# A decode kernel whose last columns of wq are loaded row by row: wider rows, other DMA engines, and part of the loads from GpSimd's queue

## The chip, the cores and the metric

One core of one Trainium2 chip runs the kernel. The metric is the device time of one execution in microseconds (us), lower is better. The engines are TensorE (PE), VectorE (DVE), ScalarE (ACT), GpSimd (POOL) and SyncE (SP); data moves between HBM and SBUF by 16 DMA engines, which loads issued from any of these queues use.

## The reference

A decode step for 8 sequences: layer norm, grouped attention over the last 2048 positions of a cache, an output projection, and a small mixer with a feed-forward part, each with a residual. For one token per sequence the shifted mixer parts are zero, so `w1` and `w2` are not needed.

```python
def _A_ref(x, k_cache, v_cache, wq, wo):         # x (8, 1, 512)
    q = (x @ wq).reshape(B, Sq, 32, 128)...       # wq (512, 4096), bf16
    k, v = the last 2048 positions of each cache  # (8, 8, 2048, 128) each, shared by 4 heads
    p = _softmax(einsum("bhqd,bhkd->bhqk", q, k) * 128 ** -0.5)
    return einsum("bhqk,bhkd->bhqd", p, v)... @ wo

def _B_ref(x, w1, w2, w3, w4):
    x1 = x + hs                                   # hs is zero for S == 1
    return x1 + _gelu(_layernorm(x1) @ w3) @ w4

h = x + _A_ref(_layernorm(x), ...)
return h + _B_ref(_layernorm(h), ...)
```

## The kernel before

**What is moved.** K and V together are 64 MB, in 32 tiles of 2 MB (128 partitions of 16 KB). With wq, wo, w3 and w4 the kernel reads 79.18 MB. All large loads are issued by SP, in an order written out by hand: `wq`, then K, K, K, V, K, V, K and so on, `wo` in three pieces, `w3`, and `w4` in three pieces. There are three buffers for K tiles and three for V tiles, so an SP issue for a later tile waits until PE is done with the tile that had its buffer.

**Order of work.** Each engine runs its own list of operations in the order in which `op` was called; waits are semaphore values. The beginning of the lists is this: POOL clears tiles (`memset`), makes `iota_f`, and computes `rstd` for the layer norm (lines 231 and 232), after DVE's statistics of x (229, 230). DVE makes `xln_b` from it (234), then constants out of `ident_f` (237 to 252), then copies the transposed x (`xlnT`). PE multiplies it by `wq` (`pe_q`), the result is evicted to `qrow2` (323, 326) and turned (`q_turn`). Only then PE transposes the first K tiles (`pe_T`, line 383), and the attention runs on in a pipeline: transposed K (`evict`), scores (`pe_QK`), softmax, P times V (`pe_PV`), batch by batch. The end is the output projection, the layer norm, `w3`, gelu, `w4` (line 732) and the store.

**How wq lies in SBUF.** The 512 rows of wq are laid as four consecutive rows to a partition, 128 partitions, in `wbig`. The last `QF` columns of the last of these four rows are not loaded with the rest. These 128 short rows are loaded by several small loads into another tile, `wqF`, which uses room that w3 takes later. `FILL` lists them: number k, the group of partitions, and the slot n among `NF` = 3 slots of `wqF`. A load with k covers 4k rows. Because these rows lie in other partitions than the rest of wq, PE needs the matching elements of x in the same order: DVE copies them out (`xlnP`, line 282), PE transposes them (`pe_fT`), DVE copies them to `xlnF` (292), and `pe_qF` adds the products of `xlnF` and `wqF` to those of `pe_q`, in the same PSUM bank `S_ps`.

In the list before, `QF` is 1152 (rows of 2304 bytes), there are six small loads, all on SP's queue behind the large one, and only bank 1 of the two needs `pe_qF`. Line 207 is the line in the helper `dma` under which all loads stand.

Of the kernel before, what the change touches and what calls it, by code (L numbers as in the profile page):

```python
# [21 lines left out]
F = 1792  # L22
FC = F // 128
FG = FC // 2
KC = D // 128
EPS = 1e-5
# [53 lines left out]
def bass_sequential_preLN__sliding_block_cached__mixer_s_mlp__decode_kernel(  # L80
# [23 lines left out]
    with es:  # L104
        sb = lambda shape, dtype, name: es.enter_context(nc.sbuf_tensor(name, shape, dtype))
        ps_t = lambda shape, dtype, name: es.enter_context(nc.psum_tensor(name, shape, dtype))
        S = lambda name: es.enter_context(nc.semaphore(name))


        iota_f = sb([128, 128], dt.float32, "iota_f")  # L110
        ident_f = sb([128, 128], dt.float32, "ident_f")
        ident_b = sb([128, 128], dt.bfloat16, "ident_b")
# [8 lines left out]
        w3_sb = sb([128, KC, F], dt.bfloat16, "w3_sb")  # L121
        w4_sb = sb([128, FC, D], dt.bfloat16, "w4_sb")
# [19 lines left out]
        xlnF = sb([KF, NF, 32], dt.bfloat16, "xlnF")  # L142
        xlnP = sb([B, 4 * sum(k for k, _, _ in FILL)], dt.bfloat16, "xlnP")
        wqF = w3_sb[0:KF, 2:4, :].rearrange("p a n -> p (a n)")[:, 0:NF * QF].rearrange("p (s n) -> p s n", s=NF)
        xlnT = sb([128, KC, 32], dt.bfloat16, "xlnT")
        qrow = sb([128, 2, 512], dt.bfloat16, "qrow")

# [1 line left out]
        qblk = sb([128, 2, G, 2, QE], dt.bfloat16, "qblk")  # L149
# [46 lines left out]

        sem_k = [S(f"sem_k{i}") for i in range(NK)]
        sem_v = [S(f"sem_v{i}") for i in range(NV)]
        sem_wf = S("sem_wf")
# [5 lines left out]
        def dma(eng, dst, src, sem, *waits):  # L205
            def f(e):
                e.dma_start(dst, src).then_inc(sem, 16)  # L207
            eng.op(f, *waits, inc=False)


        dma(AC, x_sb[:], A_x.rearrange("b s d -> (b s) d"), sem_x)
# [9 lines left out]
        e_ones = PO.op(lambda e: e.memset(ones_f[:], 1.0))  # L221
        e_mz = PO.op(lambda e: e.memset(mblk[:], 0.0))
        e_lz = PO.op(lambda e: e.memset(lblk[:], 1.0))
        e_qz = PO.op(lambda e: e.memset(qblk[:], 0.0))
        e_warm = AC.op(lambda e: e.activation(scratch[:, 1:2], scratch[:, 0:1], ACT.Exp), e_scr)

        e_idb = DV.op(lambda e: e.tensor_single_scalar(ident_b[:], iota_f[:], 0.0, ALU.is_equal), e_iota)
        e_idf = DV.op(lambda e: e.tensor_single_scalar(ident_f[:], iota_f[:], 0.0, ALU.is_equal))
        e = DV.op(lambda e: e.bn_stats(st6[:, :], x_sb[:, :]), X)
        e = DV.op(lambda e: e.bn_aggr(mv[:, :], st6[:, :]), e)  # L230
        e = PO.op(lambda e: e.tensor_scalar(rstd[:, :], mv[:, 1:2], EPS, None, ALU.add), e)
        e = PO.op(lambda e: e.tensor_tensor(rstd[:, :], rstd[:, :], half[0:B, 0:1], ALU.pow), e)
# [36 lines left out]
        qT_ps = (o_rows, sm)  # L269
        fT_ps = pT_ps[:, 128:128 + NF * B]  # L270

        def fills():
            at = 0
            for k, h, n in FILL:
                yield k, slice(32 * h, 32 * h + 4 * k), n, at, slice(at, at + 4 * k)
                at += 4 * k

        def q_rows():
            for k, rows, n, at, where in fills():
                a = xln_b[:, :]  # L280
                cols = bass.AP(tensor=a.tensor, offset=a.offset + KC * at + KC - 1, ap=[a.ap[0], [KC, k], [KC * k, 4]])
                e_xP = DV.op(lambda e, cols=cols, where=where: e.tensor_copy(
                    xlnP[:, where].rearrange("b (e a) -> b e a", a=4), cols))

            def pe_fT(e):
                for k, rows, n, at, where in fills():
                    ins = e.matmul(fT_ps[rows, n * B:(n + 1) * B], xlnP[:, where], ident_b[0:B, 0:B],
                                   is_transpose=True, tile_position=(0, rows.start))
                return ins
            e = PE.op(pe_fT, e_xP)  # L290
            for k, rows, n, at, where in fills():
                e_fT = DV.op(lambda e, rows=rows, n=n: e.tensor_copy(xlnF[rows, n, 0:B], fT_ps[rows, n * B:(n + 1) * B]),
                             e, e_fz)
            out = []
            for j in range(2):
                def pe_q(e, j=j):
                    for kc in range(KC):
                        for u in range(4):
                            n = (4 * j + u) * R * DH
                            size = R * DH if kc < KC - 1 else max(0, min(R * DH, H * DH - QF - n))  # L300
                            if size:
                                ins = e.matmul(S_ps[j][32 * u:32 * (u + 1), 0:size], xlnT[:, kc, :], wq_v[:, kc, n:n + size],  # L302
                                               start=(kc == 0), stop=(kc == KC - 1 and size == R * DH),
                                               tile_position=(0, 32 * u), skip_group_check=True)
                    return ins

                def pe_qF(e):
                    for n in range(NF):
                        for u in range(4):
                            w = (u - 4) * R * DH + QF  # L310
                            lo = max(0, -w)
                            if lo < R * DH:
                                ins = e.matmul(S_ps[1][32 * u:32 * (u + 1), lo:R * DH], xlnF[:, n, :],
                                               wqF[:, n, w + lo:w + R * DH], start=False, stop=(n == NF - 1),
                                               tile_position=(0, 32 * u), skip_group_check=True)
# [12 lines left out]
                out.append(e)  # L328
            return out, e_q
# [431 lines left out]
        def load_wq():  # L761
            size = KC * H * DH - QF
            dma(SP, wbig[:, 0:size], A_wq.rearrange("(p k) n -> p (k n)", k=KC)[:, 0:size], sem_wq)
            for k, rows, n, at, where in fills():
                dma(SP, wqF[rows, n, :],
                    bass.AP(tensor=A_wq.tensor, offset=A_wq.offset + (KC * at + KC - 1) * H * DH + H * DH - QF,
                            ap=[[KC * H * DH, k], [KC * k * H * DH, 4], [1, QF]]), sem_wf, e_wz if n else None)
# [59 lines left out]
```

## Time and profile before

| | |
|---|---|
| median of 3 runs | 192.94 us (192.86 to 194.09) |
| the profiled execution | 193.02 us, its span 191.6 us |
| PE busy | 153.1 us (80%) |
| DVE, ACT, POOL busy | 116.5, 95.6, 13.7 us |
| read from HBM | 79.18 MB, 413 GB/s over the span |
| DMA queue of SP (q1) | 97.3% of 16 engines' span |

Times in the profile are counted from the start of the span. A row of the timeline gives start, length, engine, line, operation, output and inputs, number of instructions, and in brackets how long the engine had been idle and what released it. A row of the chain that ended last gives start, length and what ran. "SPq" is an issue of a load by SP; it is not the moving of the data. "DMA share" and the digits of the DMA line tell how busy the 16 DMA engines were.

### The profile page before, as it was taken

To read this page: it belongs to the slowest core of one execution; us is meant where nothing else is said; L and a number is where in the kernel's file an instruction comes from. 1 tells how busy PE (TensorE), PEld (TensorE's weight loads), DVE (VectorE), ACT (ScalarE), POOL (GpSimd) and SP (SyncE) were. 2 spreads that over 40 slices of the span, in tenths; PEclk is the share of its full clock that TensorE was granted. 3 is DMA by queue.
4 is the path that set the end of the run, shared out by engine and by line. 5 is a ranking of instruction groups with operands and counts; after the bars stand their busy time and mean duration, and the time that the engine had idled before them with its cause. 6 is when DMAs were issued, how large, how long until landed. Compare 5 with 4: busy or idle time off the path is not lost.

```text
span 191.6 us, 3183 instructions
## 1 busy us (share of the span) xinstructions
PE 153.1 (80%) x1326; PEld 94.7 (49%) x1333; DVE 116.5 (61%) x259; ACT 95.6 (50%) x124; POOL 13.7 (7%) x37
## 2 busy tenths in 40 slices
PE   0049999598988988699978887889798895797895
PEld 0013866375556554465555455545554562343552
DVE  2733455834499368655885587558855886657423
ACT  3002667638357727284469255924782676340341
POOL 8400200100010001000100010002000000000040
PEclk9999999957999999789999999999999999699999
DMA  6999999999999999999999999999999999999991
GB/s 224 452 400 431 434 414 434 438 429 431 428 424 434 424 434 434 433 421 431 431 434 421 434 434 434 424 431 428 429 428 431 438 424 431 428 431 415 413 406 74
DMA packets 6477, 79.38 MB, mean 414 GB/s; under 512 B 688, under 2 KB 704, under 8 KB 1856
## 3 DMA queue, kind: packets, MB, share of 16 engines
q1 hardware_dynamic: 6448, 79.18, 97.3%
q8 instruction: 10, 0.16, 0.3%
q14 instruction: 3, 0.02, 0.0%
q10 hardware_dynamic: 16, 0.01, 0.0%
HBM read 79.18 MB, written 0.01 MB: 413 GB/s over the span
## 4 chain that ended last, share of the span: by engine, by line
DMA 55%; PE 20%; SPq 8%; DVE 8%; ACT 6%; issue 1%
DMA knat<-in_A_k_cache_dram 29%; DMA vnat<-in_A_v_cache_dram 11%; DMA w_sb<-in_B_w_dram 10%; SPq L207 8%; PE kT_ps L383 8%; DMA wbig<-in_A_wq_dram 6%; ACT kT_sb L393 3%; ACT pT_sb L472 3%; PE o_rows L504 3%; PE S_ps L504 3%; DVE kT_sb L395 2%; PE S_ps L302 2%; DVE oacc L516 2%; PE S_ps L408 2%; DVE omask L514 1%
## 5 line engine op out<-in xcount | busy, mean ns | idle before, releaser
L393 ACT ACTIVATE kT_sb<-kT_ps 128x1024 bf16<-128x1024 bf16 x64 | 65.6, 1025 | 54.9 <-PE kT_ps L383 54.7
L383 PE MATMUL kT_ps<-turn_f,knat 128*128 128x128 f32 x512 | 77.1, 291 | 13.8 <-DMA knat<-in_A_k_cache_dram 8.7
L383 PEld LDWEIGHTS kT_ps<-turn_f,knat 128*128 128x128 f32 x512 | 59.5, 147 | 35.0 <-issue 13.0
L395 DVE COPY kT_sb<-kT_ps 128x1024 bf16<-128x1024 bf16 x64 | 43.8, 685 | 25.4 <-PE kT_ps L383 25.2
L408 PE MATMUL S_ps<-kT_sb,qblk 128*32 128x512 bf16 x256 | 26.1, 401 | 2.7 <-ACT kT_sb L393 1.0
L504 PE MATMUL o_rows<-vnat,pT_sb 128*64 128x512 bf16 x128 | 16.5, 402 | 4.9 <-ACT pT_sb L472 4.9
L472 ACT ACTIVATE pT_sb<-o_rows,own_f 128x512 bf16<-128x512 f32 x28 | 17.7, 693 | 1.6 <-PE S_ps L408 1.2
L516 DVE TENSOR_REDUCE oacc<-omask 128x128 f32<-128x512 f32 x14 | 14.9, 1064 | 0.5
L504 PE MATMUL S_ps<-vnat,pT_sb 128*64 128x512 bf16 x112 | 13.4, 382 | 0.8 <-DMA vnat<-in_A_v_cache_dram 0.8
L504 PEld LDWEIGHTS o_rows<-vnat,pT_sb 128*64 128x64 bf16 x128 | 8.4, 114 | 11.3 <-issue 7.7
L350 POOL COPY qblk<-qT 64x64 bf16<-64x64 bf16 x16 | 5.0, 311 | 119.4 <-PE S_ps L408 106.4
L408 PEld LDWEIGHTS S_ps<-kT_sb,qblk 128*32 128x32 bf16 x256 | 6.6, 93 | 11.7 <-issue 6.9
L514 DVE TENSOR_TENSOR omask<-o_rows,own_s 128x512 f32<-128x512 f32 x7 | 4.8, 692 | 12.2 <-PE o_rows L504 12.2
L514 DVE TENSOR_TENSOR omask<-S_ps,own_s 128x512 f32<-128x512 f32 x7 | 4.8, 692 | 8.8 <-PE S_ps L504 8.8
L504 PEld LDWEIGHTS S_ps<-vnat,pT_sb 128*64 128x64 bf16 x112 | 5.8, 110 | 7.3 <-issue 2.0
L440 ACT ACTIVATE E_sb<-S_ps,negM 128x512 f32<-128x512 f32 x8 | 5.5, 689 | 6.5 <-DVE negM L436 6.5
L323 ACT ACTIVATE w_sb<-S_ps 128x512 bf16<-128x512 f32 x2 | 1.1, 594 | 11.4 <-PE S_ps L302 11.4
L259 PE MATMUL sm<-ident_b,xln_b 8*128 8x8 bf16 x4 | 0.3, 174 | 8.0 <-DVE xln_b L234 8.0
L529 PE MATMUL sm<-oacc,sel_o 128*128 128x256 f32 x16 | 6.1, 466 | 0.6 <-DVE oX L536 0.6
L431 DVE TENSOR_REDUCE mblk<-S_ps 128x1 f32<-128x512 f32 x8 | 5.5, 682 | 0.8 <-PE S_ps L408 0.8
L559 ACT ACTIVATE orow<-kT_ps 128x512 bf16<-128x512 f32 x1 | 0.6, 597 | 10.3 <-PE kT_ps L553 10.3
L453 DVE STREAM_TRANSPOSE PT_sb<-P_sb 128x512 bf16<-128x512 bf16 x8 | 5.6, 703 | 0.0
(118 smaller groups left out, 102.2 us busy)
## 6 DMA issues: line engine op xcount, KB each, us to landing
knat<-in_A_k_cache_dram SPq DMA_DIRECT2D x16, 2048.0 KB, 18.4
vnat<-in_A_v_cache_dram SPq DMA_DIRECT2D x15, 2048.0 KB, 20.1
wbig<-in_A_wq_dram SPq DMA_DIRECT2D x1, 3808.0 KB, 11.6
wbig<-in_A_wo_dram SPq DMA_DIRECT2D x2, 1024.0 KB, 22.5
knat<-in_A_v_cache_dram SPq DMA_DIRECT2D x1, 2048.0 KB, 19.8
wbig<-in_A_wo_dram SPq DMA_DIRECT2D x1, 2048.0 KB, 24.0
w_sb<-in_B_w_dram SPq DMA_DIRECT2D x1, 1792.0 KB, 29.9
w_sb<-in_B_w_dram SPq DMA_DIRECT2D x1, 1024.0 KB, 31.9
```

The source lines that it names most:

```text
L207: e.dma_start(dst, src).then_inc(sem, 16)
L383: ins = e.matmul(kT_ps[i % 2][:, n * 256:(n + 1) * 256].bitcast(dt.float32), knat[:, j % NK, c * DH:(c + 2) * DH].bitcast(dt.float32), tur ...
L393: e_lo[i] = AC.op(lambda e: e.activation(kT_sb[:, i % NKT, 0:W // 2], kT_ps[i % 2][:, 0:W // 2], ACT.Copy), e_Tlo[i], e_QK.get(i - NKT))
L395: e_hi[i] = DV.op(lambda e: e.tensor_copy(kT_sb[:, i % NKT, W // 2:W], kT_ps[i % 2][:, W // 2:W]), e_Thi[i], e_QK.get(i - NKT))
L408: ins = e.matmul(S_ps[b % 2][32 * t:32 * (t + 1), :], qblk[:, b % 2, KQ * q + t, half, at:at + H], kT[:, :, t, :, half], start=(q == 0 and ...
L431: e = DV.op(lambda e: e.tensor_reduce(mblk[:, 0:1], S_ps[b % 2][:, :], AX.X, ALU.max), e_QK[G * b + G - 1], e_mz)
L453: e_PT[b] = DV.op(lambda e: e.transpose(PT_sb[:, :], P_sb[:, :]), e_P[b], e_wide.get(b - 1))
L472: e_pT[b, t] = AC.op(lambda e: e.activation(pT_sb[:, b % 2, :, H * t:H * (t + 1)], bank[:, :].rearrange("p (n y) -> p n y", n=NN), ACT.Cop ...
L504: ins = e.matmul(bank[64 * u:64 * (u + 1), :], pT_sb[:, b % 2, n, :].rearrange("p (x q) -> p q x", q=NQ)[:, q, :], v_tile(m)[:, n * 512:(n ...
L514: free[at] = DV.op(lambda e: e.tensor_tensor(omask[:, :, :], bank.rearrange("p (s d) -> p s d", s=NS), own, ALU.mult), e_PV[m], e_acc.get( ...
L516: e_acc[m] = DV.op(lambda e: e.tensor_reduce(acc, omask[:, :, :].rearrange("p s d -> p d s"), AX.X, ALU.add), free[at], e_O.get(b - 2))
L529: e_O[b] = PE.op(lambda e: e.matmul(O_ps, sel_o[:, :], oacc[:, b % 2, :, :].rearrange("p q d -> p (q d)"), start=True, stop=True), e_acc[N ...
```

## The change

`QF` grows from 1152 to 2560, so each of the 128 short rows has 5120 bytes, and the large load of wq has 27,648 bytes per partition, not 30,464. `wqF` gets 128 partitions and moves to the end of a common tile `w34` of w3 and w4. `FILL` has ten entries, each with its queue, k, first partition, number of partitions, first slot and number of slots. Three stay on SP's queue, behind the large load. Seven go to POOL's queue; three of these are reads of 16 elements per row into a new tile `step`, which nothing reads, with k of 4, 2 and 1. Large entries of both queues wait until `wqF` has been cleared, now by a POOL memset for one slot and a DVE memset for the other two.

POOL's seven loads stand in its list after `iota` and ahead of the two `rstd` operations; the other POOL memsets go behind those. DVE's list now begins with four memsets, then the statistics of x, then the two `ident` tiles. `pe_q` runs for both banks, then `pe_qF` for both; each waits for both semaphores. The matching copies into `xlnP` are seven, the transposes three, the copy into `xlnF` one.

```diff
-QF = 1152
-FILL = ((8, 0, 0), (8, 1, 0), (8, 0, 1), (3, 1, 1), (3, 0, 2), (2, 1, 2))
+QF = 2560
 NF = 3
-KF = 64
+FILL = (("SP", 8, 0, 32, 0, 1), ("SP", 3, 32, 12, 0, 1), ("SP", 2, 0, 8, 1, 1),
+        ("PO", 4, 0, 0, 0, 0), ("PO", 1, 48, 4, 0, 3), ("PO", 2, 0, 0, 0, 0), ("PO", 2, 60, 8, 0, 3),
+        ("PO", 4, 68, 16, 0, 2), ("PO", 1, 0, 0, 0, 0), ("PO", 2, 88, 8, 0, 1))
...
+        def load_fill(eng):
+            row, off = KC * H * DH, A_wq.offset + KC * H * DH - QF
+            sem = sem_wp if eng is PO else sem_wf
+            gone = 0
+            for who, k, part, slots, count, ns, at in fills():
+                if (who == "PO") != (eng is PO):
+                    continue
+                if count == 0:
+                    m = 2 if k == 1 else k
+                    r = 3 if k == 1 else 1
+                    dma(eng, step[gone:gone + m, 0:r * 16].rearrange("p (r n) -> p r n", r=r),
+                        bass.AP(tensor=A_wq.tensor, offset=off, ap=[[row, 3], [3 * row, 2], [1, 16]] if k == 1 else
+                                [[row, k], [1, 16]]), sem)
+                    gone += m
+                else:
+                    m = NF if k == 1 else k
+                    dma(eng, wqF[part, slots, :], bass.AP(tensor=A_wq.tensor, offset=off + at * row,
+                                                          ap=[[row, m], [m * row, count // m], [1, QF]]), sem, *e_wz)
...
-        e_fz = PO.op(lambda e: e.memset(xlnF[:], 0.0))
-        e_wz = PO.op(lambda e: e.memset(wqF[:, 1:NF, :], 0.0))
-        e_xz = PO.op(lambda e: e.memset(xlnT[:], 0.0))
+        wide = lambda t: t.rearrange("p s n -> p (s n)").bitcast(dt.float32)
+        e_wz = [PO.op(lambda e: e.memset(wide(wqF[:, 2:NF, :]), 0.0)),
+                DV.op(lambda e: e.memset(wide(wqF[:, 0:2, :]), 0.0))]
+        DV.op(lambda e: e.memset(wide(xlnF[:, :, :]), 0.0))
+        DV.op(lambda e: e.memset(xlnP[:, :, :], 0.0))
+        e_xz = DV.op(lambda e: e.memset(wide(xlnT[:, :, :]), 0.0))
         e_iota = PO.op(lambda e: e.iota(...))
+        load_fill(PO)
...
-                e_q = PE.op(pe_q, e_xT, (sem_wq, 16))
-                if j == 1:
-                    e_q = PE.op(pe_qF, e_fT, (sem_wf, 16 * len(FILL)))
+                PE.op(pe_q, e_xT, (sem_wq, 16))
+                filled.append(pe_qF)
+            for j in range(2):
+                e_q = PE.op(filled[j], e_fT, *((sem, 16 * sum(f[0] == who for f in FILL))
+                                           for sem, who in ((sem_wf, "SP"), (sem_wp, "PO"))))
...
         def load_wq():
             size = KC * H * DH - QF
             dma(SP, wbig[:, 0:size], A_wq.rearrange("(p k) n -> p (k n)", k=KC)[:, 0:size], sem_wq)
-            for k, rows, n, at, where in fills():
-                dma(SP, wqF[rows, n, :], ..., sem_wf, e_wz if n else None)
+            load_fill(SP)
```

More of the change, by code (lines that the diff above doesn't have):

```diff
@@ L140, in bass_sequential_preLN__sliding_block_cached__mixer_s_mlp__decode_kernel @@
         rstd = sb([B, 1], dt.float32, "rstd")
-        xlnF = sb([KF, NF, 32], dt.bfloat16, "xlnF")
-        xlnP = sb([B, 4 * sum(k for k, _, _ in FILL)], dt.bfloat16, "xlnP")
-        wqF = w3_sb[0:KF, 2:4, :].rearrange("p a n -> p (a n)")[:, 0:NF * QF].rearrange("p (s n) -> p s n", s=NF)
+        xlnF = sb([128, NF, 32], dt.bfloat16, "xlnF")
+        xlnP = sb([B, 128, NF], dt.bfloat16, "xlnP")
+        step = sb([8, 48], dt.bfloat16, "step")
+        wqF = w34[:, KC * F + FC * D - NF * QF:KC * F + FC * D].rearrange("p (s n) -> p s n", s=NF)
         xlnT = sb([128, KC, 32], dt.bfloat16, "xlnT")
@@ L198, in bass_sequential_preLN__sliding_block_cached__mixer_s_mlp__decode_kernel @@
         sem_v = [S(f"sem_v{i}") for i in range(NV)]
[L199 removed]
+        sem_wf, sem_wp = S("sem_wf"), S("sem_wp")
         sem_x, sem_wq, sem_w3, sem_out = (S(n) for n in ("sem_x", "sem_wq", "sem_w3", "sem_out"))
@@ L208, in dma, with fills @@
             eng.op(f, *waits, inc=False)
+        def fills():
+            at = 0
+            for who, k, part, count, slot, ns in FILL:
+                yield who, k, slice(part, part + count), slice(slot, slot + ns), count * ns, ns, at
+                at += count * ns
+        def load_fill(eng):
[16 more added lines that the diff above has]
+                                                          ap=[[row, m], [m * row, count // m], [1, QF]]), sem, *e_wz)
         dma(AC, x_sb[:], A_x.rearrange("b s d -> (b s) d"), sem_x)
@@ new lines, in bass_sequential_preLN__sliding_block_cached__mixer_s_mlp__decode_kernel @@
+        e_bn = DV.op(lambda e: e.bn_aggr(mv[:, :], st6[:, :]), e)
+        e_idb = DV.op(lambda e: e.tensor_single_scalar(ident_b[:], iota_f[:], 0.0, ALU.is_equal), e_iota)
+        e_idf = DV.op(lambda e: e.tensor_single_scalar(ident_f[:], iota_f[:], 0.0, ALU.is_equal))
+        e = PO.op(lambda e: e.tensor_scalar(rstd[:, :], mv[:, 1:2], EPS, None, ALU.add), e_bn)
+        e = PO.op(lambda e: e.tensor_tensor(rstd[:, :], rstd[:, :], half[0:B, 0:1], ALU.pow), e)
+        e_qz = PO.op(lambda e: e.memset(qblk[:], 0.0))
@@ L222, in bass_sequential_preLN__sliding_block_cached__mixer_s_mlp__decode_kernel @@
         e_mz = PO.op(lambda e: e.memset(mblk[:], 0.0))
         e_lz = PO.op(lambda e: e.memset(lblk[:], 1.0))
[L224 to L229, printed above, removed]
@@ L230, in bass_sequential_preLN__sliding_block_cached__mixer_s_mlp__decode_kernel @@
-        e = DV.op(lambda e: e.bn_aggr(mv[:, :], st6[:, :]), e)
-        e = PO.op(lambda e: e.tensor_scalar(rstd[:, :], mv[:, 1:2], EPS, None, ALU.add), e)
-        e = PO.op(lambda e: e.tensor_tensor(rstd[:, :], rstd[:, :], half[0:B, 0:1], ALU.pow), e)
+        e_ones = PO.op(lambda e: e.memset(ones_f[:], 1.0))
         e_oz = PO.op(lambda e: e.memset(oW[:], 0.0))
@@ L270, in bass_sequential_preLN__sliding_block_cached__mixer_s_mlp__decode_kernel @@
         fT_ps = pT_ps[:, 128:128 + NF * B]
[L272 to L276, printed above, removed]
-        def q_rows():
-            for k, rows, n, at, where in fills():
[L280 to L283, printed above, removed]
+        def q_rows():
+            for who, k, part, slots, count, ns, at in fills():
+                if count:
+                    a = xln_b[:, :]
+                    m = NF if k == 1 else k
+                    to = xlnP[:, part, slots]
+                    if ns == NF:
+                        to = to.rearrange("b p s -> b (p s)").rearrange("b (m q) -> b m q", m=m)
+                        ap = [a.ap[0], [KC, m], [KC * m, count // m]]
+                    else:
+                        to = to.rearrange("b (m q) s -> b m q s", m=m)
+                        ap = [a.ap[0], [KC, m], [KC * m * ns, count // m // ns], [KC * m, ns]]
+                    cols = bass.AP(tensor=a.tensor, offset=a.offset + KC * at + KC - 1, ap=ap)
+                    e_xP = DV.op(lambda e, cols=cols, to=to: e.tensor_copy(to, cols), e_xln)
             def pe_fT(e):
-                for k, rows, n, at, where in fills():
-                    ins = e.matmul(fT_ps[rows, n * B:(n + 1) * B], xlnP[:, where], ident_b[0:B, 0:B],
-                                   is_transpose=True, tile_position=(0, rows.start))
+                for n in range(NF):
+                    ins = e.matmul(fT_ps[:, n * B:(n + 1) * B], xlnP[:, :, n], ident_b[0:B, 0:B], is_transpose=True)
                 return ins
             e = PE.op(pe_fT, e_xP)
-            for k, rows, n, at, where in fills():
-                e_fT = DV.op(lambda e, rows=rows, n=n: e.tensor_copy(xlnF[rows, n, 0:B], fT_ps[rows, n * B:(n + 1) * B]),
-                             e, e_fz)
+            e_fT = DV.op(lambda e: e.tensor_copy(xlnF[:, :, 0:B], fT_ps.rearrange("p (n b) -> p n b", n=NF)), e)
+            filled = []
             out = []
@@ L763, in load_wq @@
             dma(SP, wbig[:, 0:size], A_wq.rearrange("(p k) n -> p (k n)", k=KC)[:, 0:size], sem_wq)
[L764 to L767, printed above, removed]
+            load_fill(SP)
         def load_w3():
```

20 lines of the change are left out of this document (10 added, 10 removed).

## The prediction

> **What bounds the kernel now.** I read the slices and queues of the page first, then the chain that ended last, then the timeline of the start, then two stretches of it.
>
> ```profile
> DMA  6999999999999999999999999999999999999991
> GB/s 224 452 400 431 434 414 434 438 429 431 428 424 434 424 434 434 433 421 431 431 434 421 434 434 434 424 431 428 429 428 431 438 424 431 428 431 415 413 406 74
> ...
> q1 hardware_dynamic: 6448, 79.18, 97.3%
> q8 instruction: 10, 0.16, 0.3%
> q14 instruction: 3, 0.02, 0.0%
> ```
>
> The DMA engines are busy from the first slice to the last but one, at 413 GB/s over the span: the kernel streams 79.18 MB and computes beside it. Two small queues fetch instructions, 13 packets in all.
>
> ```profile
> 24.78 13.97 DMA knat<-in_A_k_cache_dram
> 38.75 0.04 issue
> 38.79 1.97 PE kT_ps L383 x8
> ...
> 170.00 19.17 DMA w_sb<-in_B_w_dram
> 189.17 0.04 issue
> 189.22 0.32 PE S_ps L732 x8
> ```
>
> The chain ends on the last piece of `w4`, landed at 189.17; what follows takes 2.43 us to the span's 191.6. That load was issued 19 us before, so no issue limits it: the queues do. A load has landed when the slowest of 16 DMA engines is done. The trace's record of when each engine reported the end of that last load shows the engines apart (us after the first, which was at 186.20):
>
> ```
> 0.00 0.01 0.88 0.97 1.38 1.43 1.45 1.58 1.61 1.97 2.24 2.32 2.34 2.73 2.91 2.97
> ```
>
> Their mean is 1.67. Were all 16 to end together, the load would land 2.97 - 1.67 = 1.30 us earlier; that is the most any redistribution of the same bytes can win.
>
> **Where the spread comes from.** The same record for the first K tile (first report at 16.91) has eight engines at 0.00 to 0.20, five at 0.86 to 1.27, one at 2.04, two at 2.23 and 2.36. That is the six fill loads, whose first numbers in FILL are 8, 8, 8, 3, 3, 2: their semaphore has 38 updates, which is one for each of 32 engines' shares and one for each of the six issues. So the first number is the count of engines, four rows each: eight engines carry no row of 2304 bytes, five carry 12, one 20, two 24. Following the record from tile to tile, an engine then jumps now and then by 1.4 to 1.7 us, ten jumps beside the ten q8 packets, and by 0.5 to 1.0 beside the three q14 packets. At the end I read: of the eight empty engines two were never hit (0.00, 0.01), five once (1.38 to 1.61), one twice (2.97); of the five with 12 rows two never (0.88, 0.97), three once (2.24 to 2.34); of the last three one never (1.97), two by the small kind (2.73, 2.91).
>
> **The change, part by part.**
>
> *Bytes per engine.* Successive K tiles are 4.87 us apart for 128 KB on each engine, so a row of 5120 bytes costs 0.19 us and one of 2304 bytes 0.086 us. `wbig` loses 8 x 2816 bytes on every engine, 0.84 us. By the new list the SP loads put 12 rows on engines 0 and 1, 8 on 2, 4 on 3 to 7. The POOL loads name 4, 1, 2, 2, 4, 1, 2 engines: 16 together, four of real rows, three of 16-element reads into `step`, which nothing reads. No trace here shows a load from POOL. If each takes the engines that follow those of the load before it, beginning at engine 0, they put 12 rows on engine 4, 12 on 7 and 8, 8 on 9 to 12, 4 on 14 and 15, none on 13. Then 4 and 7 hold 16 rows, 3, 5, 6 hold 4, 13 none, and this fits the hits above: two of the five unhit, three hit; one of the eight hit twice. In the coordinates of the list above (0.19 us x rows + hits - 0.84):
>
> - 4, 7: 3.04 - 0.84 = 2.20
> - 9 to 12, hit once: 1.52 + 1.50 - 0.84 = 2.18
> - 13, hit twice: 2.97 - 0.84 = 2.13
> - 0, 1 with a small hit: 2.28 + 0.50 - 0.84 = 1.94
> - 8, unhit: 1.44; 3, 5, 6: 0.76 + 1.40 - 0.84 = 1.32; 2: 0.68; 14, 15: -0.08 or 1.42
>
> Their mean is again about 1.66, as it must be. The last is 2.20 where it was 2.97: **0.77 us won**. A hit that falls on 4 or 7 instead makes 3.6, 0.6 us lost.
>
> The Trainium skill, "DMA: Bandwidth & Descriptors", section "Why a DMA increments its semaphore by 16 and not by 1", states just such a turn for loads from POOL (k consecutive engines from a round-robin cursor), and the lowest-numbered k for SP's; SP's part agrees with the 38 reports, the rest no run here shows yet.
>
> *Added small packets.* Report packets in the record take 9 ns; 7 POOL loads on at most 16 engines each add up to 0.06 us per engine, three SP loads fewer take some back. The reads into `step` are a few short packets. Between 0 and 0.15 us; I take 0.05.
>
> *The start.* POOL's queue now stands so: memsets, iota, seven loads, then the two `rstd` operations on which the layer norm, and so everything of q, waits.
>
> ```profile
> 1.18 4.74 SPq L207 DMA_DIRECT2D w_sb<-in_A_wq_dram  x6
> ...
> 6.36 0.57 POOL L232 TENSOR_TENSOR rstd<-rstd,half 8x1 f32<-8x1 f32 x1
> ...
> 10.59 0.24 PE L287 MATMUL sm<-ident_b,xlnP 8*32 8x8 bf16 x6 [2.28 <-DVE xlnP L282]
> ...
> 12.33 3.59 PE L302 MATMUL S_ps<-wbig,xlnT 128*32 128x512 bf16 x30 [1.50 <-DMA wbig<-in_A_wq_dram]
> ...
> 15.85 1.47 PE L313 MATMUL S_ps<-w_sb,xlnF 64*32 64x128 bf16 x9
> ...
> 24.78 0.54 SPq L207 DMA_DIRECT2D knat<-in_A_k_cache_dram  x1
> ```
>
> Before, rstd ended at 6.93 and the transposes at 10.83, 3.9 us later, with 1.5 us to spare before `wbig` landed. Now: the POOL memset of 1280 elements by L224's 1.42 us for 1600, 1.2 us, done at 2.0; iota to 2.4. The second POOL load and SP's first wait for the DVE memset of 2560 elements, bounded by L395's 0.69 us per 1024 (1.7) and L217's 2.02 per 2304 (2.3, on POOL): I take 2.5, done at 3.3. SP then issues three fills of 0.79 us and the first K tile at 5.7, against 5.96 before: no loss there. Six more POOL loads follow. An issue costs between SP's 0.40 and, by the slowest small POOL row (L709, 1.68), some 2 us. I take 1.0, near SP's 0.79 for the same kind of load. Then POOL is free at 9.3, rstd done at 10.2, PE ready at 14.2 instead of 12.33.
>
> PE then has 27 matmuls against `wbig` (0.117 each by 3.49 us for 30), 3.2 us, and 15 against the fills (0.16 by 1.47 for 9), 2.4 us, to 19.8 instead of 17.32. The fills may hold it longer: a queue beside SP's gets its turn between packets of 0.6 to 1.0 us, so 12 rows issued at 5 to 6 land near 18. I take q **2.5 to 3.6 us late**; the two evictions and turns behind it are as before.
>
> *What hides it.* Queued behind q on PE are the transposes of the first K tiles, and behind the first tile's last transpose SP waits to issue the fourth (24.78). Before that, V0 must drain: its first engine reported at 31.50, 30.7 now for an engine without rows. A first packet starts 1.0 us after issue (the first at 1.73, issued 0.72). So the fourth K tile may be issued 30.7 - 0.3 - 1.0 - 24.8 = 4.6 us later without a gap. PE itself catches up here:
>
> ```profile
> 36.00:38.70 2.70, 0.65 (x5) 0.23 (x5) 2.07 (x6) 1.09 (x3) 0.00 (x0) 0.91 1.04 446
> ```
>
> It worked 0.65 us (first column behind the length) of 2.70 there, waiting for the fourth tile. So 2 us are given back by 38.8 and the rest by the next such waits. Later loads are issued 14 to 21 us ahead (the chain's 13.97, 20.66, 20.23), so nothing else is late. Cost 0.
>
> *Sum.* 193.02 (the profiled execution; 191.6 span and 1.42 around it; the median of the runs is 192.94, 0.08 less) - 0.77 + 0.05 + 0 = **192.3**.
>
> **Rivals.**
>
> *POOL's loads are spread evenly* (4.75 rows on each of 16): 0 and 1 end at 16.75 x 0.19 + 0.5 - 0.84 = 2.84, the twice-hit engine at 0.90 + 2.13 = 3.03. Time 192.9 to 193.1: no change. For it: every large load here uses all 16. Against: the fills of before did go to 8, 3 and 2. The Trainium skill's rule in "DMA: Bandwidth & Descriptors", "Issuing engines are not separate DMA queues" (the engine that starts a load changes only issue time), points this way.
>
> *The turn begins elsewhere, or the instruction reads fall elsewhere.* Beginning at engine 9, engines 0 and 1 get 24 rows: 4.56 + 0.5 - 0.84 = 4.22, so 193.02 + 1.25 = 194.3; milder shifts or a hit on 4 or 7, 193.4 to 193.7. For it: neither place is shown by the page. Against: the hits fit so well.
>
> *POOL's loads go to the lowest engines, as SP's do*: engine 0 holds 12 + 12 + 12 + 8 + 4 = 48 rows, 9.1 + 0.5 - 0.84 = 8.8, 198.8.
>
> *q comes too late* (slower): the place is POOL's seven issues ahead of rstd, the price 6 us per us of issue. At 2 us each, rstd ends at 16.2, q is 2.5 + 6.0 = 8.5 us late, the fourth K tile 3.9 us behind its queue. The emptiest engine idles that long and ends at 2.13 + 3.9 = 6.0: 193.02 + 3.1 = 196.1. It decides from 5.5 us of delay on (2.13 + 0.9 = 3.0), an issue of 1.5 us. For it: DVE's L227 took 1.69 us beside POOL's 1.42 us memset where L239, a plain copy of the same 128x128, took 0.25 once POOL's memset was over, so the two engines get in each other's way at the start. The Trainium skill, "SBUF — State Buffer", section "SBUF: two separate sides", has POOL's descriptors starve beside some DVE operations. Against: DVE has little to do between 5 and 10 us now.
>
> **How the numbers follow.** Forecast (191.7 to 192.8) 0.58; even spread 0.14; other turn or other hits 0.12; late q 0.12; lowest engines 0.04. What a measurement of this kernel can tell from no change is about 1%, 191.0 and 194.9. No case reaches 191.0, since balance is worth 1.30 at most; I leave 0.03 for a surprise. Slower: most of late q and the lowest engines, 0.14. Within 1%: 0.83. The range runs from perfect balance, 191.7, to the worst of the shifted turns, 194.3, and leaves out the lowest engines and most of late q.
>
> **What would show it.** Right: the 16 reports of the last load within 2.4 us, their mean about where it was (187.9), landing near 188.4; rstd at 9 to 11, q done 2 to 4 us later, the fourth K tile issued by 29 and no gap in the DMA slices. Wrong: a spread of 3 or more with the mean unchanged (turn or hits), a mean later by over 0.2 (overhead or a gap), POOL's loads over 1.5 us apart, DMA slices below 9 near 30 us.

## The result and the profile after

The change makes the kernel slower: 211.22 us (median of six runs, 210.38 to 211.78) against 192.91 (six runs, 192.81 to 194.09), a ratio of 1.0933 with a 95% interval of 1.0896 to 1.097. That is 18.3 us more; the forecast was 192.3 and its range ended at 194.3. The profiled execution took 211.57 us, its span 210.2. One execution of all the runs below, one of e10's four, is left out: it took 215.84 us at a granted TensorE clock of 0.675, where the other three had 0.93 to 0.94.

Slices and queues of the page after, to be held against the same lines of before:

```profile
DMA  7999996007999999999999999999999999999990
GB/s 254 423 356 369 377 335 259 22 3 277 421 432 433 421 436 433 421 433 435 424 427 436 424 433 430 433 430 427 429 433 421 436 440 415 430 440 411 414 391 35
...
q1 hardware_dynamic: 6353, 78.79, 90.1%
q0 software_dynamic: 736, 0.39, 0.7%
q8 instruction: 10, 0.16, 0.3%
q14 instruction: 3, 0.02, 0.0%
```

A slice is 5.26 us. The seventh to the tenth read 6, 0, 0 and 7 where before had nines; in the eighth and ninth, 36.8 to 47.3 us, next to nothing is moved. From the eleventh slice on the rate is that of before. Already in the third to the sixth it is 335 to 377 GB/s and not 400 to 434, with DMA busy. And there is a new queue, q0, that of POOL's loads. It carries 0.39 MB, but in 736 packets.

The chain that ended last, whose earlier part now goes through POOL:

```profile
7.51 30.60 DMA w<-in_A_wq_dram
38.24 2.73 PE S_ps L344 x15
...
187.22 20.61 DMA w<-in_B_w_dram
207.83 0.04 issue
207.88 0.32 PE S_ps L764 x8
```

The last of POOL's seven loads is issued at 7.51 and lands 30.60 us later, at 38.1. It is 40 KB. PE's products with `wqF` (line 344) begin only then, and the timeline shows what follows:

```profile
7.51 0.57 POOL L210 DMA_DIRECT2D w<-in_A_wq_dram  x1
8.42 0.58 POOL L260 TENSOR_TENSOR rstd<-rstd,half 8x1 f32<-8x1 f32 x1
14.54 3.17 PE L334 MATMUL S_ps<-wbig,xlnT 128*32 128x512 bf16 x27
38.24 2.72 PE L344 MATMUL S_ps<-w,xlnF 128*32 128x512 bf16 x15 [20.52 <-DMA w<-in_A_wq_dram]
47.60 0.53 SPq L210 DMA_DIRECT2D knat<-in_A_k_cache_dram  x1
```

PE stood 20.52 us with the products against `wbig` done at 17.71. The fourth K tile, which waits in SP's list until PE has turned the first, is issued at 47.60 (24.78 before). Two stretches show the two halves of this (columns: length, busy time and count of PE, its weight loads, DVE, ACT, POOL, then granted clock, DMA share, GB/s):

```profile
18.00:28.00 10.00, 0.00 (x0) 0.00 (x0) 0.00 (x0) 0.00 (x0) 0.00 (x0) 1.00 1.01 366
39.20:48.60 9.40, 9.00 (x64) 5.95 (x56) 4.54 (x8) 5.07 (x6) 1.26 (x4) 1.00 0.01 2
```

First all compute engines wait for the DMA queues, which move 366 GB/s; then PE works 9.00 of 9.40 us and the DMA queues wait for it, at 2 GB/s. Neither lost stretch overlaps the other.

The mean over the 16 DMA engines of the report that a load has ended shows where the delay stays:

| us | before | after | difference |
|---|---|---|---|
| first V tile | 32.37 | 36.13 | +3.76 |
| fourth K tile | 37.22 | 54.76 | +17.54 |
| last piece of w4 | 187.87 | 205.50 | +17.63 |
| the same, last engine | 189.17 | 207.83 | +18.66 |

Of the mean, everything is lost by the fourth K tile, and next to nothing is gained or lost in the 150 us behind it. The last engine comes 18.66 later, 1.0 more than the mean; that is the spread of the engines, taken up under "Balance" below.

### The profile page after: what moved, and what is told of

Its sections match the earlier page's. It is cut to its first block, busy times and chain, and to the rows that moved or that the text cites. A ratio compares the mean times of both kernels' runs of the same rounds, so it can differ in the third digit from the quotient of the medians.

```text
span 210.2 us, 3188 instructions
## 1 busy us (share of the span) xinstructions
PE 151.1 (72%) x1326; PEld 92.6 (44%) x1333; DVE 118.3 (56%) x259; ACT 95.5 (45%) x124; POOL 17.2 (8%) x42
## 4 chain that ended last, share of the span: by engine, by line
DMA 53%; PE 19%; DVE 11%; SPq 8%; ACT 5%; issue 2%; POOL 2%
DMA knat<-in_A_k_cache_dram 19%; DMA w<-in_A_wq_dram 15%; DMA w<-in_B_w_dram 10%; DMA vnat<-in_A_v_cache_dram 10%; PE kT_ps L415 9%; SPq L210 8%; ACT pT_sb L504 3%; PE o_rows L536 3%; PE S_ps L536 3%; DVE kT_sb L427 3%; PE S_ps L440 2%; ACT kT_sb L425 2%; DVE oacc L548 2%; PE S_ps L344 1%; DVE mblk L463 1%
## 5 line engine op out<-in xcount | busy, mean ns | idle before, releaser
L415 PE MATMUL kT_ps<-turn_f,knat 128*128 128x128 f32 x512 | 74.3, 283 | 9.9 <-DVE kT_sb L427 5.3
L415 PEld LDWEIGHTS kT_ps<-turn_f,knat 128*128 128x128 f32 x512 | 56.8, 142 | 30.7 <-issue 13.0
L536 PE MATMUL o_rows<-vnat,pT_sb 128*64 128x512 bf16 x128 | 17.1, 412 | 5.3 <-ACT pT_sb L504 5.3
L355 ACT ACTIVATE w<-S_ps 128x512 bf16<-128x512 f32 x2 | 1.1, 594 | 36.9 <-PE S_ps L344 36.9
L344 PE MATMUL S_ps<-w,xlnF 128*32 128x512 bf16 x15 | 2.7, 624 | 20.5 <-DMA w<-in_A_wq_dram 20.5
L358 DVE TENSOR_SCALAR w<-S_ps 128x512 bf16<-128x512 f32 x2 | 1.3, 686 | 26.2 <-PE S_ps L344 26.2
L536 PE MATMUL S_ps<-vnat,pT_sb 128*64 128x512 bf16 x112 | 13.9, 392 | 0.7 <-DMA vnat<-in_A_v_cache_dram 0.7
L344 PEld LDWEIGHTS S_ps<-w,xlnF 128*32 128x32 bf16 x15 | 0.8, 125 | 22.4 <-issue 22.4
## 6 DMA issues: line engine op xcount, KB each, us to landing
knat<-in_A_k_cache_dram SPq DMA_DIRECT2D x16, 2048.0 KB, 18.2
wbig<-in_A_wo_dram SPq DMA_DIRECT2D x2, 1024.0 KB, 22.6
```

What stands on the lines that cost most here:

```text
L344: ins = e.matmul(S_ps[j][32 * u:32 * (u + 1), :], xlnF[:, n, :], wqF[:, n, w:w + R * DH], start=False, stop=(n == NF - 1), tile_position=( ...
L415: ins = e.matmul(kT_ps[i % 2][:, n * 256:(n + 1) * 256].bitcast(dt.float32), knat[:, j % NK, c * DH:(c + 2) * DH].bitcast(dt.float32), tur ...
L536: ins = e.matmul(bank[64 * u:64 * (u + 1), :], pT_sb[:, b % 2, n, :].rearrange("p (x q) -> p q x", q=NQ)[:, q, :], v_tile(m)[:, n * 512:(n ...
```

## The experiments

**The theory, and what stands against it.** The trace's record of q0 has 736 packets, 46 for each of 16 engines: 76 rows of 5120 bytes, 7 short reads into `step`, 112 reports (7 loads by 16 engines), and packets that are neither, called fillers here, 526 of 4 bytes and 15 of 24. This is what comes out, to the packet, if a POOL load puts as many packets on *every* engine as its busiest engine has rows. For the seven loads these are 1, 12, 1, 12, 8, 1 and 4, in all 39, and 7 reports make 46. The change's three SP loads on 8, 3 and 2 engines left no fillers: the 661 packets of 4 bytes in SP's queue are all reports, 13 of them of these three loads. A filler takes 9 ns itself, but follows its predecessor by 1.04 us while `wbig` is moved and by 0.65 to 0.8 while K tiles are: one packet of SP's, then one of POOL's. From 6.49, the first, 46 such turns end with the last report at 38.1: 0.69 us each. Theory **turns**: the time is the number of turns times SP's packet, and what is late is q. The Trainium skill, "DMA: Bandwidth & Descriptors", section "Queues, rings and completion order", says that each DMA engine goes round its queues and takes a whole packet from one before the next; the 46 turns agree.

Rivals: **bytes** (POOL's rows of 5120 bytes are slow in themselves), **slow queue** (POOL's queue takes some 0.65 us for a packet, whatever is beside it), and **order** (the reordered start of POOL's and DVE's lists, not the loads).

Runs e3, e4, e5, e6, e7, e11 and e12 are single; their times stand beside a kernel before of 192.9 to 193.2 on the same chip. The others have four or ten executions each.

**e1, no load of POOL's.** All 128 rows by one SP load on 16 engines, everything else as changed.

```diff
-FILL = (("SP", 8, 0, 32, 0, 1), ... ("PO", 2, 88, 8, 0, 1))
+FILL = (("SP", 16, 0, 128, 0, 1),)
```

> All 128 rows of 5120 bytes in one load on SP's queue over 16 engines, 8 rows each; POOL issues none. The rest of the change stays, the order at the start too. Turns (each POOL load puts as many packets on all 16 DMA engines as its busiest has rows, and each such packet waits for one packet of SP's queue): with no POOL packet q is done near 20 us, no gap, and the engines differ by the instruction reads alone: 192.9 to 194.5. Slow queue (POOL's queue needs some 0.65 us for a packet whatever is beside it) and bytes (POOL's queue is slow in moving its 0.39 MB): the same. Start order (the new order of memsets, statistics and matmuls costs the time): about 211.

Measured 196.18 us, ratio 1.0191 (1.0152 to 1.0229). The fourth K tile is issued at 23.69, and the DMA line has no gap:

```profile
DMA  7999999999999999999999999999999999999980
23.69 0.54 SPq L208 DMA_DIRECT2D knat<-in_A_k_cache_dram  x1
```

The 15 us are gone, so the order at the start is not the cause. The 2% that stay were not expected; they are taken up under e15 and e17.

**e2, the same bytes through POOL in one load on 16 engines.**

```diff
+FILL = (("SP", 16, 0, 48, 0, 1), ("PO", 16, 48, 80, 0, 1))
```

> 48 rows from SP over 16 engines (3 each), 80 rows in one POOL load over 16 engines (5 each). Turns: 5 rows and one report, 6 packets for each engine, landed by 11 to 13 us, no gap: 193 to 194.5. Slow queue: 6 packets are soon done too, 193 to 194.5. Bytes: 0.41 MB take as long as the change's 0.39, landed after 35 us, about 210.

Measured 196.13, ratio 1.0179 (1.0121 to 1.0237), again above what was expected. Queue and timeline:

```profile
q0 software_dynamic: 96, 0.41, 0.7%
```

```profile
16.57 1.95 PE L342 MATMUL S_ps<-w,xlnF 128*32 128x512 bf16 x15
```

As many bytes as in the change (0.41 MB for 0.39), but 6 packets per engine: the last is reported at 15.5 (11 to 13 was expected), PE does not wait (no bracket), and the fourth K tile is issued at 24.93. Bytes through POOL are not the cause.

**e3, POOL's loads with short rows.** POOL's real rows are cut to 16 elements; the other elements of these rows are left out.

```diff
-                    dma(eng, wqF[part, slots, :], ... ap=[[row, m], [m * row, count // m], [1, QF]]), sem, *e_wz)
+                    w = 16 if eng is PO else QF
+                    dma(eng, wqF[part, slots, 0:w], ... ap=[[row, m], [m * row, count // m], [1, w]]), sem, *e_wz)
```

> The seven POOL loads with the same engines and rows, but 16 elements (32 bytes) of each row and not 2560; the other elements of these rows are left out of the computation. Turns: the 46 packets of each engine are the same, landed at 35 to 38 us, 207 to 211. Slow queue: the same. Bytes: landed near 10 us, 193 to 194.

Measured 192.34. The queue's line shows why this tells nothing between the theories:

```profile
q0 software_dynamic: 224, 0.01, 0.1%
```

14 packets per engine, not 46: rows of 32 bytes are joined, one packet and one report per load and engine. The last was reported at 17.0. The premise of the expectation, equal packets with fewer bytes, did not hold; 14 turns without a wait fit turns, and fewer bytes fit as well.

**e4, about half the turns.** Each POOL load of real rows is dealt to twice as many engines: rows per engine 6, 6, 4 and 2, with reports and short reads 28 packets.

```diff
-("PO", 1, 48, 4, 0, 3) ("PO", 2, 60, 8, 0, 3) ("PO", 4, 68, 16, 0, 2) ("PO", 2, 88, 8, 0, 1)
+("PO", 2, 48, 4, 0, 3) ("PO", 4, 60, 8, 0, 3) ("PO", 8, 68, 16, 0, 2) ("PO", 4, 88, 8, 0, 1)
```

> Each of the four POOL loads of rows over twice the engines, so 6, 6, 4, 2 rows on the busiest and not 12, 12, 8, 4: 28 packets for each engine and not 46, the same bytes. Turns: some 5 of the 28 pass beside the large load of wq, 23 at 0.72 us after 11.5, landed near 28 us; the gap shrinks by 10 us and the engines lose less: 198 to 202. Slow queue: landed near 6.5 + 28 x 0.68 = 26 us, the same time. Bytes: 211.

Measured 201.56, as turns has it, and a slow queue too; e5 and e7 part these two. The last report is at 28.5 (28 turns of 0.78 us from 6.59), the fourth K tile issued at 37.61:

```profile
28.61 2.72 PE L344 MATMUL S_ps<-w,xlnF 128*32 128x512 bf16 x15 [11.04 <-DMA w<-in_A_wq_dram]
```

**e5 and e6, shorter packets on SP's queue.** Every K and V tile in four loads of 4096 bytes per partition instead of one of 16,384: e5 in the kernel after, e6 in the kernel before.

```diff
+        def pieces(dst, src, sem, *waits):
+            n = CQ * DH // SPLIT
+            for x in range(SPLIT):
+                dma(SP, dst[:, x * n:(x + 1) * n], src[:, :, x * n:(x + 1) * n], sem, *waits)
```

> The change, with every K and V tile loaded in four loads of 4096 bytes per partition and not one of 16384. Turns: after the large load of wq (11.5 us) some 41 of the 46 packets are left, each beside a packet of 0.15 us and not 0.7: landed at 18 to 21 us, fourth K tile hardly late: 194 to 199. Slow queue: landed near 38 us as before, 209 to 213.

> The kernel before with the same splitting of K and V tiles, as the measure for the run above. All theories: 192.9 to 194.5; more reports and more SP issues, which stay below the 4.87 us of a tile.

e5 took 203.12, e6 197.1, both more than was expected. Splitting alone costs 4 us (e6, one run), so e5 has to be read against e6. In e5 there are 46 packets per engine as in the change, but the last is reported at 22.6 instead of 38.1, and the wait is short:

```profile
22.72 2.72 PE L345 MATMUL S_ps<-w,xlnF 128*32 128x512 bf16 x15 [4.99 <-DMA w<-in_A_wq_dram]
```

So the length of the packets beside it sets a turn's price. Of the 18.3 us the change cost, 6.0 are left over e6's own time.

**e7, nothing beside POOL's loads.** SP holds back its first K load until POOL's are in.

```diff
+                (sem_wp, 16 * sum(f[0] == "PO" for f in FILL)) if j == 0 else None)
```

> The change, with SP's first K load waiting until all POOL loads have landed, so that only the large wq load and three fills stand beside them. Turns: some 5 of the 46 packets pass by 11.5 us, the others then need no turn, 0.05 to 0.2 us each, landed at 14 to 18 us, then K; the DMA engines idle 3 to 7 us: 196 to 201. Slow queue: landed near 38 us, K 26 us late: 217 to 222.

Measured 200.45. The last of the 46 packets is reported at 16.84, and PE goes on at once:

```profile
17.12 2.31 PE L344 MATMUL S_ps<-w,xlnF 128*32 128x512 bf16 x15
```

The same seven loads, issued at the same times, take a third of the time when no K tile is beside them. POOL's queue is not slow in itself, nor is it held up by what POOL and DVE do at the start, for their lists are those of the change. What e7 loses, it loses in the empty queue ahead of its first K tile, issued at 16.86 instead of 6.07.

**e9, the change's order with the loads of before.** `QF` 1152 and six SP loads of before in the changed code and its order.

```diff
-QF = 2560
+QF = 1152
+FILL = (("SP", 8, 0, 32, 0, 1), ("SP", 8, 32, 32, 0, 1), ("SP", 8, 0, 32, 1, 1), ("SP", 3, 32, 12, 1, 1),
+        ("SP", 3, 0, 12, 2, 1), ("SP", 2, 32, 8, 2, 1))
```

> The change's code and order at the start, with QF and the six SP loads of the kernel before; POOL issues no load. What is left of the change is the order of memsets, statistics and constants, and rows in 128 partitions. If the cost is POOL's packets alone: 192.5 to 193.5. If the new order costs something of its own (it could hide behind the wait in the run with all rows on SP): 194 to 196.

Measured 192.84, ratio 0.9988 (0.9957 to 1.0019). The order costs nothing that this interval shows.

Together:

| kernel | POOL packets per engine | beside them | last POOL report | fourth K tile issued | time |
|---|---|---|---|---|---|
| after | 46 | `wbig`, then 16 KB packets | 38.1 | 47.60 | 211.2 |
| e4 | 28 | `wbig`, then 16 KB packets | 28.5 | 37.61 | 201.6 |
| e2 | 6 | `wbig`, then 16 KB packets | 15.5 | 24.93 | 196.1 |
| e5 | 46 | `wbig`, then 4 KB packets | 22.6 | 32.60 | 203.1 (e6: 197.1) |
| e7 | 46 | `wbig`, no K tile | 16.8 | 30.07 | 200.5 |

**e11 and e12, more in the queue.** Is it enough to have more tiles issued before the fourth K? Both take the order K, K, K, V, V, V, K for the first tiles, so that two more V tiles cover the wait; e11 with the change's loads, e12 with those of e4.

```diff
-        for kind in "QKKK" + 9 * "VK" + "VKKVKVKVVVOVOO":
+        for kind in "QKKKVVVKK" + 7 * "KV" + "KKVKVKVVVOVOO":
```

> The change, with SP's second and third V loads issued ahead of its fourth K load, which has to wait; their buffers are free from the start. Turns, the time lost as a gap in SP's queue: the queue has two tiles more, 9.7 us, and is dry by 49 us, when the fourth K load (47.6) is there: the gap of 10 us goes, what is left is dearer packets and a PE that is 23 us late: 197 to 202. If the time were lost otherwise (POOL's packets slowing the engines throughout): 207 to 211.

> The same order of SP's loads with POOL's loads of rows over twice the engines (28 packets). q done near 33, the fourth K load issued at 37.6, the queue dry at 47 only: no gap and PE 13 us late: 193.5 to 197. If the lateness of q counts in full, gap or not: 201.

e11 took 207.19, 4 us less than the change, and e12 201.52, as much as e4: little or nothing is gained, against the expectation that two tiles more would cover 10 us more. Both times lie where the other reading on record has them; for e11 that reading was packets that slow the engines throughout, and the trace shows gaps instead. In e12 the first gap is gone, but the queue runs dry later, at the fourth V tile: it waits for PE's first product with V and is issued at 62.82 (before 49.52), and its mean report is 9.6 us after that of the load ahead, where 4.9 is the usual distance:

```profile
62.82 0.54 SPq L210 DMA_DIRECT2D vnat<-in_A_v_cache_dram  x1
```

In e11 the delay is spread over several gaps, the last 4.6 us at the fourth V tile. So a late start of PE is passed on to each later load that waits for PE; more issued loads move the gap, they do not remove it. The only reserve is the distance between PE and the queue, about 5 us: in e12 the fourth V tile is issued 13.3 us late and the last load ends 8.4 late on average, in e11 19.6 and 14.7.

**What a POOL load costs beside the lateness: e8, e10, e13, e14, e16.** These five put loads like the seven into the kernel *before*, from some 20 us after the start, where nothing waits for them. They read extra bytes, into a tile that nothing reads.

```diff
+LATE = ((4, 1, 4, 1), (4, 3, 3, 4), (2, 1, 2, 1), (8, 3, 2, 12), (16, 2, 4, 8), (2, 3, 3, 2), (8, 1, 2, 4))
...
+        for parts, ns, m, c in LATE:
+            dma(PO, thin[at:at + parts, 0:ns, 0:n], ... [[row, m], [m * row, c], [1, n]] ..., sem_wp)
```

e8: n is 16 throughout. e10: real rows have 2304 elements (4608 bytes). e13: as e10, from adjoining rows of HBM. e14: as e10, but `LATE = ((80, 1, 16, 5),)`, one load on 16 engines. e16: as e10, into the partitions that the change uses.

> The kernel before, with seven more POOL loads of the change's engines and rows, 32 bytes a row, into a tile that nothing reads, issued from about 22 us on, when nothing waits for them; 46 packets for each engine beside the K and V tiles. It measures what the packets cost the DMA engines apart from their lateness. In the change SP's packets of 16384 bytes took about 0.72 us and not 0.61 beside them, and the first V tile landed 3.8 us later on average. Turns with a price (each packet costs its engine some 0.08 us): 196 to 197.5. Lateness alone: 192.9 to 193.5.

> The kernel before with the seven late POOL loads once more, now with rows of 4608 bytes, into room that w4 takes later, so that each engine has 46 packets again and not 14, with 0.35 MB more to read (0.8 us at 430 GB/s). It measures what the packets cost the DMA engines when nothing waits for them. If a packet costs 0.08 us beside its bytes: 46 x 0.08 + 0.8 = 4.5, with the uneven rows 197 to 198.5. If lateness is all: 193.5 to 195.

> The late seven POOL loads of wide rows (46 packets for each engine), but read from one dense piece of wq, 4608 bytes apart, and not from every fourth row, 32 KB apart. With rows 32 KB apart the reports of the last load came 3.7 us later on average than in the kernel before, 0.8 of it for the bytes. If the 2.9 us are a price of packets: the same, 199 to 201.5, mean report near 191.5. If they come from reading rows 32 KB apart: mean report near 188.7, and with the uneven rows 195 to 197.5.

> One late POOL load of 80 rows of 4608 bytes, 32 KB apart, over 16 engines: 6 packets for each engine and not 46, nearly the same bytes. Price of packets (0.063 us each): 0.4 + 0.9 for the bytes, 194 to 195, mean report 188.9 to 189.3. Price of rows that lie 32 KB apart: mean report near 191.5, 196 to 198.

> The late seven POOL loads of wide rows as before (46 packets for each engine, rows 32 KB apart), but into the partitions that the change uses for them (48, 60, 68, 88 and on) and not into 4 and on. If rows are dear because an engine writes where another engine's K tile goes, and the change's partitions are the engines' own: mean report from 191.57 to 188.7 to 189.5, 194.5 to 196.5. If the price is that of the packets: mean report 191 to 191.6, 198 to 200.5.

| run | time | ratio (95%) | packets per engine | mean end of the last load |
|---|---|---|---|---|
| e8 | 193.32 | 1.0022 (0.999 to 1.0054) | 14 | 188.02 (+0.15) |
| e10 | 200.34 | 1.0338 (1.027 to 1.0406) | 46 | 191.57 (+3.7) |
| e13 | 198.91 | 1.0328 (1.0257 to 1.0399) | 46 | 190.96 (+3.1) |
| e14 | 195.21 | 1.0119 (1.006 to 1.0177) | 6 | 190.10 (+2.2) |
| e16 | 198.8 | 1.0284 (1.0224 to 1.0344) | 46 | 191.96 (+4.1) |

e8 missed its premise, short rows being joined again. e10 shows a second cost: its 76 rows are 0.8 us of bytes, yet the mean end is 3.7 us later. Neither the distance of the rows in HBM (e13) nor the partitions (e16) makes it, and with 6 packets it is still 1.4 us beyond the bytes (e14; 2.23 less 0.86 for its 80 rows). That is about 0.07 us for each of 46 packets in e16, (4.1 - 0.8) / 46, but 0.2 for each of 6 in e14, so it is no fixed price per packet, and what it is stays open. It does not bear on the 18.3 us: in the change a delay of the same size is seen on the first V tile, +3.76, and the queue runs dry behind that tile, so that it only shortens the gap that follows.

**The 2% of e1 and e2: e15 and e17.** In e1 the row record shows a median of 335 ns, and up to 404, for a row of 5120 bytes, against 196 expected from the prediction's 0.19. e15 is e1 with the 128 rows from adjoining places (these are not the values of wq that q needs). e17 is e1 with row n in partition n.

```diff
-  ap=[[row, m], [m * row, count // m], [1, QF]]     # e1: m = 16, eight neighbouring partitions to an engine
+  ap=[[QF, m], [m * QF, count // m], [1, QF]]       # e15
+  ap=[[row, 128], [1, QF]]                          # e17
```

> All 128 rows in one SP load over 16 engines again, now read from one dense piece of wq, 5120 bytes apart; these are not the values the computation needs, so that part of q is made from others. Rows 32 KB apart took 335 to 400 ns on all engines at once where 196 ns is usual, and the K packets after them up to 1140 ns. If the distance is the reason: 196 ns again, K0 1.2 us earlier, 193.5 to 195. If it is 16 engines reading short rows at once, whatever the distance: 195.5 to 197.

> All 128 rows in one SP load over 16 engines, but row n of the 128 to partition n in plain order (the pattern of the K tiles), where the earlier run dealt them out 8 partitions in a row to an engine. If short rows are dear where engines write to each other's partitions: 196 ns a row and not 335 to 400, the first K tile's mean report near 17.8 and not 19.0, 193 to 194.8. If 16 engines with short rows are dear anyhow: 195.5 to 197.

e15 took 196.43, ratio 1.0167 (1.01 to 1.0233), its rows 354 ns: the distance in HBM is not it. e17 took 194.61, ratio 1.0061 (1.003 to 1.0093), its rows 196 ns. What differs from e1 is which engine has which rows and writes which partitions; as e15 speaks against the place of the rows, the partitions are the likelier reason, which is argued and not shown. The Trainium skill, "DMA: Bandwidth & Descriptors", section "The descriptor swizzle", gives for a load of 128 partitions which partitions belong to an engine, and says that each then writes a port of its own. e17's 196 ns against e1's 335 fit that; the ports themselves no run here shows.

e17 is also the kernel with no balancing of the DMA engines at all. Its mean end is 187.82 (before 187.87), its last engine 189.69 (189.17). So in the one profile of each the balancing of the kernel before is worth 0.5 us at the end of the queue. The times lie 1.6 us apart (194.61 to 193.0); where the rest comes from is open.

## Why the prediction was wrong

**The step that failed** is the sentence under "The start": "a queue beside SP's gets its turn between packets of 0.6 to 1.0 us, so 12 rows issued at 5 to 6 land near 18". The price of a turn was right: 1.04 us beside `wbig`, 0.65 to 0.8 beside K tiles. The number of turns was not: it counted the 12 rows of one load on the engines that get them. It is 46, since all seven loads share one queue on each engine and each adds its busiest engine's count to *all* engines, with a report. With 46 turns of 0.69 us from 6.49 on, a price within its own 0.6 to 1.0, the rows would have been found to land at 38.1 and not near 18. "q 2.5 to 3.6 us late" became 22.4 (line 344 at 38.24 instead of 15.85), and the term "Cost 0" became 17.6 us of the 18.3.

**Cover.** The fourth K tile was forecast to have 4.6 us to spare. In the change it was issued 22.8 us late and the mean end moved by 17.6; in e4 12.8 and 7.6. Both leave 5.2 us absorbed. This step held: with the true issue time its 4.6 gives 22.8 - 4.6 = 18.2, where 17.6 was measured. "Nothing else is late" holds only for a delay that fits into the cover; e11 and e12 show the fourth V tile next.

**Balance.** The 0.77 us could not come, and the reason is the gap. A dry queue lets all engines begin the next load level: the reports of the fourth K tile lie within 0.54 us. What rows an engine carried before is wiped out. The reports of the last load (us after the first, at 204.37) show the instruction reads that fall after the gap, and no more:

```
0.00 0.02 0.04 0.05 0.11 0.50 0.54 1.47 1.55 1.63 1.66 1.67 1.78 1.83 1.84 3.46
```

As I read them: five engines unhit, two with the small kind, eight hit once by 1.5 to 1.8, one twice. The second hit on that one is the last of the ten instruction reads, at 205.8; the load ahead of it still ended within 1.86 us. Which engine a read falls on, no run here explains. The spread is 3.46, where at most 2.4 was forecast and 2.97 was before. So the turn of POOL's loads over the engines, and the term worked out from it, was neither shown right nor wrong.

**Small packets.** 0.05 us was taken for them by their own length of 9 ns. The length is right; what was left out is that each waits for its turn.

**The start.** POOL's issues took 0.57 to 0.75 us each (1.0 taken), rstd ended at 9.00 (10.2), PE was ready at 14.54 (14.2), SP's first K tile went out at 6.07 (5.7), the 27 matmuls took 3.17 (3.2), the DVE memset 2.19 (2.5). These hold.

**The rivals.** "q comes too late" was the right mechanism from q on: fourth K tile, dry queue, a shift of the whole stream. But its place was POOL's issues ahead of rstd, which were short; what is late is the landing of their rows, so its price of 196.1 was too small by 15. It had a chance of 0.12. In a sentence beside "even spread" the prediction named the Trainium skill's "DMA: Bandwidth & Descriptors", section "Issuing engines are not separate DMA queues", by which another issuing engine changes issue time alone. With one load on 16 engines that agrees: 1.0179 with 80 rows on POOL (e2), 1.0191 without any (e1). It does not tell of the 1.0933 with seven POOL loads on few engines. The fillers that make their turns are in POOL's queue alone; a run with the same seven loads on SP was not made.

Two of the signs that the prediction listed under "wrong" appeared: digits of the DMA line below 9 and a mean later by over 0.2. POOL's issues over 1.5 us apart, the sign of the rival's place, did not, apart from the second load's wait for the DVE memset (2.24 to 4.27).

## What to carry to other kernels

Before a load goes to a second queue, count the packets that it puts on its busiest DMA engine and one for its report, add those of all loads on that queue, and multiply by the time of one packet of the stream beside it: behind 16 KB packets a 40 KB load landed after 30.6 us. Ask then what the first waiting consumer holds back in an in-order list, how many us of loads are issued ahead of it, and which load waits next; beyond that cover, some 5 us here, each us counted in full. The rows themselves cost little when one POOL load dealt them to all 16 engines (e2). A balance of DMA engines worth a us was lost here when the queue once ran dry.

## What the runs showed of the hardware

- By the count of q0's packets, a POOL load on one engine with 12 rows puts 12 packets on all 16; the fillers have 4 bytes. Rows of 32 bytes are joined to one packet per load and engine (14 instead of 46 per engine in e3 and e8).
- POOL's first packet moves 4.25 us after its load's issue began (2.24 to 6.49), SP's 1.0 us after (0.72 to 1.75).
- An SP load of 128 rows of 5120 bytes takes 1.7 times as long per row (335 for 196 ns) when its pattern deals eight neighbouring partitions to an engine (e1) instead of row n to partition n (e17).
- K and V tiles in rows of 4 KB instead of 16 KB cost 4 us (197.1, one run).
- Late POOL loads with rows of 4608 bytes cost 1.4 to 3.3 us beyond their bytes; the cause was not found.
